# Retention and softplus feed-forward on one core: weight pieces in the order of use, one rest in four on GpSimd, two early constants' loads apart, and three idle products between the first two steps

## The chip, the cores and the metric

The kernel runs on one core of a Trainium2 chip. The metric is the device time of one execution in microseconds (us): the median of three runs of the kernel before is 893.17 us (893.16 to 894.15). The trace comes from one more execution, which took 891.85 us.

The engines are named as the profile names them: PE is TensorE's matmul, PEld its weight load, DVE is VectorE, ACT is ScalarE, POOL is GpSimd, SP is SyncE, on which all DMAs are issued here.

## The reference

```
scores = (q @ k.T) / sqrt(64)                   # 8 batches, 8 heads, 576 positions, head size 64
ret    = scores * gamma[h] ** (i - j)  (j <= i) # lower triangle with a decay per head
attn   = ret @ v
x      = attn, heads side by side               # 4608 tokens x 512
h      = x @ w_in                               # 512 x 2048
g      = max(h, 0) + log1p(exp(-|h|))           # softplus
out    = g @ w_out                              # 2048 x 512
```

All of it is float32. The weights are kept as pairs of a high and a low part, and so are x and g, so that each large product is three products in the fast format (high with low, low with high, high with high).

## The kernel before

**Attention** runs in steps: a step is one chunk of 128 tokens and two pairs of heads, so two steps make a chunk and there are 72 in all. The first eight steps are computed whole (`scores_whole`, `sums_whole`, `values_whole`), before any large product; the ninth follows half. For each the kernel loads a tile `raw` of 512 KB with k, q, k again and v, multiplies k by q (line 290), masks the result on DVE (`a_whole`, line 297), scales v on ACT (line 154), multiplies sums and values (lines 305, 327, 332), keeps a state per head that decays (lines 315 to 319), multiplies the output by a column of decays (`x`, line 344) and splits x into a high and a low part (lines 351, 352). The small constants (scales of v and the states' decay) and the columns of decays lie in the tiles of the first step, behind its data: `part0` holds k, q and the small ones, `part1` holds k, v and the columns. All constants are loaded a second time behind step 9, for the time after the opening.

**The feed-forward** runs in slots: slot i takes 512 tokens and the p-th of 16 strips of 128 hidden columns, `h` = 12 matmuls (line 367), softplus on ACT and DVE (lines 375 to 395), and one slot later `y` += 12 matmuls for the output (line 407). PE's order in a slot is: in odd slots the small products of one attention step, then `h(i)`, then `y(i-1)`. `y(i-1)` reads the low part of g first, which line 395 writes.

**The weights** come in 32 pieces of 512 columns as 64-bit floats. A piece is scaled on ACT (`weight_p`, line 440), its low word on DVE (`weight_t`, line 447), both are joined on DVE (`weight_b`, line 453), the high part is rounded on ACT (`weight_c`, line 461) and the rest is subtracted on DVE (`weight_d`, line 466). `weight_dl` also issues the load of the piece four further on. Pieces alternate: the strip of w_in, then the strip of w_out, of p = 0, 1, 2. Pieces 0 to 3 are loaded in the opening, 0 and 1 are finished there, and slot i works on pieces 2 + 2i and 3 + 2i: the rest of the first stands before the softplus sum (line 387), the rest of the second behind it. So in slot i the first `weight_dl` finishes the strip of w_in that `h(i+1)` reads, and the second the strip of w_out for `y(i)`.

The order on every engine is that of the code, written by hand; no planner sets it. Three idle products on a tile of ones (line 493) stand on PE ahead of the first scores.

Of the kernel before, what the change touches and what calls it, by code (L numbers as in the profile page):

```python
# [19 lines left out]
P = 128  # L20
# [20 lines left out]
START_WEIGHTS = 3  # L41
OPENING = 3
NOPEN = AHEAD + 2
CHUNKS = 9
FIRST_HALF = NF // 2
WBUFS = 4
NPIECE = 2 * NF
HI, LO = 0, 1
TERMS = ((LO, HI), (HI, LO), (HI, HI))


# [12 lines left out]
def retention_softplus_ffn(ctx: ExitStack, tc, first, whole, others, consts, w, out):  # L64
# [20 lines left out]

    parts = [openp.tile([P, n], F32, name=f"part{i}") for i, n in enumerate((4 * C + SMALL, 4 * C + NPAIR * C))]
    consts_sb = const.tile([P, NCONST], F32, name="consts_sb")
    mask = const.tile([P, HC], F32, name="mask")

    def constants(small, columns):  # L90

        return small[:, 0:H], small[:, H:SMALL], columns.rearrange("p (s c) -> p s c", s=NPAIR)

    constant = [constants(parts[0][:, 4 * C:], parts[1][:, 4 * C:])]
# [8 lines left out]
    place_weights(wpool, FIRST_HALF)  # L103

# [16 lines left out]
    def load_step(m):  # L121

        if m == 0:
            at = 0
            for x in parts:
                nc.sync.dma_start(x, first[:, at:at + x.shape[1]])
                at += x.shape[1]
            k, q = parts[0][:, 0:2 * C], parts[0][:, 2 * C:4 * C]
            kp, v = parts[1][:, 0:2 * C], parts[1][:, 2 * C:4 * C]
        else:  # L130
            if m < NOPEN:
                r = openp.tile([P, 8 * C if m < FIRST else RAW], F32, name=f"raw{m}")
                nc.sync.dma_start(r, whole[m - 1] if m < FIRST else others[m - FIRST])
                keys, qv = r[:, 0:KEYS], r[:, KEYS:]
            else:
                keys = rawp.tile([P, KEYS], F32, tag="keys", name="keys")
                nc.sync.dma_start(keys, others[m - FIRST][:, 0:KEYS])
                place = later["odd"] if m >= 2 * CHUNKS and m // 2 % 2 else rawp
                qv = place.tile([P, RAW - KEYS], F32, tag="qv", name="qv")
                nc.sync.dma_start(qv, others[m - FIRST][:, KEYS:])  # L140
            k, kp, q, v = keys[:, 0:2 * C], keys[:, 2 * C:], qv[:, 0:-2 * C], qv[:, -2 * C:]
        live[m] = {n: x.rearrange("p (s c) -> p s c", s=2) for n, x in dict(k=k, q=q, kp=kp, v=v).items()}

    def scale_values(m):

        if m >= NSTEP:
            return
        v = live[m]["v"].rearrange("p s (h d) -> p (s h) d", h=2)
        f = constant[0][0][:, 4 * (m % 2):4 * (m % 2) + 4]
# [46 lines left out]
    def states_out(m):  # L196
# [21 lines left out]
        if follows:  # L218
            s = att.tile([P, 2, D], F32, tag="s", name="s", bufs=4)
            if between is None:  # L220
                nc.vector.tensor_copy(s, sum1)
            else:
                nc.vector.tensor_add(s, sum1, between)  # L223
            f = constant[0][1][:, 2 * (m % 2):2 * (m % 2) + 2]
            nc.gpsimd.tensor_mul(s, s, f.unsqueeze(2).broadcast_to([P, 2, D]))  # L225
            states[m % 2] = s
# [82 lines left out]
    def state_whole(m):  # L309
        before = states.get(m % 2)  # L310
        live[m]["before"] = before
        total = live[m]["T"].rearrange("p (s d) -> p s d", s=2)
        s = att.tile([P, 2, D], F32, tag="s", name="s", bufs=4)
        if before is None:
            nc.vector.tensor_copy(s, total)
        else:
            nc.vector.tensor_add(s, total, before)
        f = constant[0][1][:, 2 * (m % 2):2 * (m % 2) + 2]
        nc.gpsimd.tensor_mul(s, s, f.unsqueeze(2).broadcast_to([P, 2, D]))
        states[m % 2] = s  # L320
# [15 lines left out]
    def values_out(m, rest):  # L336
# [6 lines left out]
        if m < FIRST:  # L343
            nc.vector.tensor_mul(x, L["O"], constant[0][2][:, pr:pr + 2])
        else:
            nc.vector.tensor_mul(x.rearrange("p s (t c) -> p s t c", t=2),  # L346
                                 L["O"].rearrange("p t (s c) -> p s t c", s=2),
                                 constant[0][2][:, pr:pr + 2].rearrange("p s (t c) -> p s t c", t=2))

# [9 lines left out]
    def hidden_mm(i, tag, cols=slice(0, T)):  # L359
# [5 lines left out]
        for a, b in TERMS:  # L365
            for kt in range(NKT):
                nc.tensor.matmul(h, ws[p][:, a, kt * P:(kt + 1) * P], xt[:, b, kt, cols],  # L367
                                 start=(n == 0), stop=(n == 3 * NKT - 1))
# [28 lines left out]
    def output_mm(i):  # L397
# [4 lines left out]
        for tt in range(CPU):  # L402
            y = ys[u][tt]
            for n, (a, b) in enumerate(TERMS):
                g = parts[tt * len(parts) // CPU]
                at = tt % (CPU // len(parts)) * P
                nc.tensor.matmul(y, g[:, a, at:at + P], ws[p][:, b, PIECE:],  # L407
                                 start=(p == 0 and n == 0), stop=(p == NF - 1 and n == 2))
# [18 lines left out]
    def load_weight(n):  # L427
        if n < NPIECE:
            wl[n] = wst.tile([P, PIECE, 2], I32, tag="wst", name="wst", bufs=WBUFS)
            nc.sync.dma_start(wl[n].rearrange("p c a -> p (c a)"), w[n // 2, n % 2])  # L430

# [23 lines left out]
    def weight_dst(n):  # L455
        cols = slice((n % 2) * PIECE, (n % 2 + 1) * PIECE)
        return ws[n // 2][:, HI, cols], ws[n // 2][:, LO, cols]

# [3 lines left out]

    def weight_d(n):
        if n in wl:
            head, rest = weight_dst(n)
            nc.vector.tensor_sub(rest, wl.pop(n)[:, :, 1].bitcast(F32), head.bitcast(F32))  # L466
# [24 lines left out]
    idle = ps_val.tile([P, 2, T], F32, tag="val", name="idle")  # L491
    for n in range(OPENING):
        nc.tensor.matmul(idle[:, 0, 0:2 * C], fill[:, 0:P], fill[:, 0:2 * C], start=True, stop=True)

# [8 lines left out]
    for m in range(2):  # L503
        next_scores(m)
        scale_values(m)
        masked_whole(m)
# [32 lines left out]
    ps_y = ctx.enter_context(tc.tile_pool(name="ps_y", bufs=1, space=PSUM, side="right"))  # L539
    constant[0] = constants(consts_sb[:, 0:SMALL], consts_sb[:, SMALL:])  # L540

# [3 lines left out]
    for i in range(NSLOT):  # L545
# [48 lines left out]
        if step and n < NPIECE:  # L594
# [6 lines left out]
            if m == NOPEN:  # L601
                open_pools.close()
                place_weights(ctx.enter_context(tc.tile_pool(name="wpool2", bufs=1)), NF)
        weight_c(n)
        weight_dl(n)
        gs[i] = [softplus_split(ab)]
# [84 lines left out]
```

## Time and profile before

| what | value |
|---|---|
| median of 3 runs | 893.17 us |
| the profiled execution | 891.85 us |
| its span, first to last instruction | 890.1 us |
| PE busy | 879.6 us (99%) |
| DVE, ACT, POOL busy | 460.1, 440.6, 144.1 us |
| mean granted TensorE clock | 0.998 of full speed |

The table gives totals over the whole span. The change lies in the opening (0 to about 23 us) and in the stretch in which the weights are still being prepared (to about 120 us), so the rows further down are from there. A timeline row gives the start, the time that it took, engine, line, operation, tiles and count, and in brackets how long the engine had been idle before and what ended that.

### The profile page before, as it was taken

What the parts mean: (1) busy time and instruction counts of PE and PEld (TensorE: products, weight loads), DVE (VectorE), ACT (ScalarE), POOL (GpSimd) and SP (SyncE); (2) the same over time, 40 slices, a digit from 0 to 9 for tenths busy, and PEclk for the clock granted to TensorE, in tenths of its full rate; (3) what the DMA queues carried; (4) which work ended last, traced back from release to release, by engine and by line L of the source; (5) the groups of instructions that cost most, each with busy time, mean ns of one, the idle gap of its engine ahead of it and who ended that gap; (6) DMA issues with size and microseconds to landing.
All of it is one profiled execution on the core that took longest, in us unless ns stands there. A gap on an engine that the chain in (4) does not pass through costs nothing.

```text
span 890.1 us, 18133 instructions
## 1 busy us (share of the span) xinstructions
PE 879.6 (99%) x7634; PEld 723.8 (81%) x7634; DVE 460.1 (52%) x875; ACT 440.6 (49%) x771; POOL 144.1 (16%) x265
## 2 busy tenths in 40 slices
PE   8999999999999999999999999999999999999998
PEld 6777778888888888888888888888888888888886
DVE  5898864445444454455444454444444544434333
ACT  6777854444544454444444454444444544444444
POOL 4221222111111111111111111111111111000000
PEclk9999999999999999999999999999999999999999
DMA  9666623111310121112111131012111211001001
GB/s 364 193 216 221 218 69 113 54 55 54 102 47 23 41 101 54 55 55 101 55 54 54 55 102 54 26 41 90 54 54 54 101 55 54 2 1 48 0 1 48
DMA packets 29313, 69.86 MB, mean 78 GB/s; under 512 B 3248, under 2 KB 3248, under 8 KB 29232
## 3 DMA queue, kind: packets, MB, share of 16 engines
q1 hardware_dynamic: 29232, 68.71, 22.9%
q8 instruction: 60, 0.98, 0.5%
q14 instruction: 21, 0.17, 0.1%
HBM read 59.26 MB, written 9.44 MB: 77 GB/s over the span
## 4 chain that ended last, share of the span: by engine, by line
PE 93%; DVE 3%; ACT 1%; DMA 1%; issue 0%; SPq 0%; DVEq 0%
PE h L367 43%; PE y L407 42%; PE sums L174 2%; PE bank L158 2%; PE bank L230 2%; PE bank L242 1%; DVE w L466 1%; DMA raw<-whole 1%; DVE g L395 1%; PE pair L290 1%; DMA wst<-w 1%; PE bank L327 0%; PE bank L305 0%; ACT ab L377 0%; ACT ab L376 0%
## 5 line engine op out<-in xcount | busy, mean ns | idle before, releaser
L367 PE MATMUL h<-xt,w 128*128 128x512 f32 (+1 forms) x1740 | 420.5, 391 | 1.9 <-DVE w L466 1.3
L407 PE MATMUL y<-w,g 128*128 128x512 f32 x1728 | 415.9, 390 | 1.2 <-DVE g L395 1.2
L407 PEld LDWEIGHTS y<-w,g 128*128 128x128 f32 x1728 | 323.7, 188 | 71.0 <-DVE g L395 4.0
L367 PEld LDWEIGHTS h<-xt,w 128*128 128x128 f32 x1740 | 322.1, 188 | 70.0 <-DVE w L466 1.7
L375 ACT ACTIVATE ab<-h 128x512 f32<-128x512 f32 (+1 forms) x145 | 86.3, 595 | 252.0 <-PE h L367 252.0
L383 DVE TENSOR_SCALAR r<-h 128x512 f32<-128x512 f32 x125 | 86.4, 692 | 211.1 <-ACT ab L375 211.1
L391 ACT CAST g<-ab 128x512 fp32r<-128x512 f32 (+1 forms) x145 | 89.5, 617 | 106.1 <-DVE ab L387 104.9
L395 DVE TENSOR_TENSOR g<-ab,g 128x512 fp32r<-128x512 f32 (+1 forms) x145 | 103.1, 711 | 69.4 <-ACT g L391 68.0
L352 POOL TENSOR_TENSOR xt<-x,xt 128x256 fp32r<-128x256 f32 x71 | 54.2, 780 | 519.7 <-ACT xt L351 519.7
L387 DVE SCALAR_TENSOR_TENSOR ab<-r,ab 128x512 f32<-128x512 f32 x125 | 89.4, 715 | 79.6 <-ACT ab L377 79.6
L376 ACT ACTIVATE ab<-ab 128x512 f32<-128x512 f32 (+1 forms) x145 | 91.2, 629 | 4.6
L377 ACT ACTIVATE ab<-ab 128x512 f32<-128x512 f32 (+1 forms) x145 | 91.2, 629 | 4.7
L351 ACT CAST xt<-x 128x256 fp32r<-128x256 f32 x72 | 27.1, 405 | 56.8 <-DVE x L346 55.4
L151 POOL TENSOR_TENSOR qv<-qv,consts_sb 128x256 f32<-128x256 f32 x61 | 41.3, 676 | 52.0 <-DMA qv<-others 51.6
L225 POOL TENSOR_TENSOR s<-s,consts_sb 128x128 f32<-128x128 f32 x55 | 24.2, 440 | 62.3 <-DVE s L223 50.1
L158 PE MATMUL bank<-qv,keys 64*64 64x64 f32 x976 | 34.0, 222 | 0.0
L346 DVE TENSOR_TENSOR x<-bank,consts_sb 128x256 f32<-128x256 f32 x64 | 24.6, 419 | 17.8 <-PE sums L174 12.3
L174 PEld LDWEIGHTS sums<-qv,keys 64*64 64x64 f32 x768 | 26.5, 134 | 8.5 <-issue 8.5
L230 PE MATMUL bank<-a,qv 64*64 64x64 f32 x976 | 32.9, 218 | 0.0
L158 PEld LDWEIGHTS bank<-qv,keys 64*64 64x64 f32 x976 | 29.4, 134 | 3.5 <-issue 3.5
L174 PE MATMUL sums<-qv,keys 64*64 64x64 f32 x768 | 32.0, 221 | 0.0
L230 PEld LDWEIGHTS bank<-a,qv 64*64 64x64 f32 x976 | 29.9, 135 | 0.4 <-issue 0.4
(84 smaller groups left out, 444.2 us busy)
## 6 DMA issues: line engine op xcount, KB each, us to landing
qv<-others SPq DMA_DIRECT2D x61, 320.0 KB, 4.1
wst<-w SPq DMA_DIRECT2D x32, 512.0 KB, 4.2
keys<-others SPq DMA_DIRECT2D x61, 256.0 KB, 3.5
out<-osb SPq DMA_DIRECT2D x36, 256.0 KB, 2.4
raw<-whole SPq DMA_DIRECT2D x7, 512.0 KB, 8.3
raw<-others SPq DMA_DIRECT2D x3, 576.0 KB, 10.7
part<-first SPq DMA_DIRECT2D x1, 512.0 KB, 3.7
part<-first SPq DMA_DIRECT2D x1, 262.0 KB, 2.7
```

The lines of the kernel that those rows point to most:

```text
L158: nc.tensor.matmul(L["S"][rows[t], h, part[s]], L["k"][rows[h], s, part[t]], L["q"][rows[h], s, part[t]], start=True, stop=True, skip_grou ...
L174: nc.tensor.matmul(L["T"][rows[h], t, part[s]], L["kp"][rows[t], s, rows[h]], L["v"][rows[t], s, rows[h]], start=True, stop=True, skip_gro ...
L230: nc.tensor.matmul(L["O"][rows[h], t, part[s]], L["v"][rows[t], s, rows[h]], L["a"][rows[t], h, s], start=clear, stop=L["states"][t] is No ...
L367: nc.tensor.matmul(h, ws[p][:, a, kt * P:(kt + 1) * P], xt[:, b, kt, cols], start=(n == 0), stop=(n == 3 * NKT - 1))
L375: nc.scalar.activation(ab, h, AF.Abs)
L376: nc.scalar.activation(ab, ab, AF.Exp, scale=-1.0)
L377: nc.scalar.activation(ab, ab, AF.Ln, bias=1.0)
L383: nc.vector.tensor_scalar_max(r, h, 0.0)
L387: nc.vector.scalar_tensor_tensor(ab, h, 0.0, ab, op0=ALU.max, op1=ALU.add)
L391: nc.scalar.copy(g[:, HI], ab)
L395: nc.vector.tensor_sub(g[:, LO], ab, g[:, HI].bitcast(F32))
L407: nc.tensor.matmul(y, g[:, a, at:at + P], ws[p][:, b, PIECE:], start=(p == 0 and n == 0), stop=(p == NF - 1 and n == 2))
```

## The change

Five edits, all in the first 120 us:

1. The first step's data come in two tiles of 256 KB without constants. The small constants (128 rows of 48 bytes) are a DMA of their own between the two, the columns of decays (256 KB) a DMA behind the load of step 1 and ahead of that of step 2. The second load of all constants behind step 9 goes.
2. Three more idle products (`BETWEEN`) follow the scores of step 0 on PE.
3. The weights' pieces are numbered in the order in which PE reads them: w_in of 0, w_in of 1, w_out of 0, w_in of 2, w_out of 1 and so on (`_piece`). The slots' code is the same, so the second `weight_dl` of slot i now finishes what `h(i+2)` reads, and the first one what `y(i)` reads.
4. In even slots the rest of the second piece is subtracted on POOL instead of DVE (`weight_dl(n, nc.vector if i % 2 else nc.gpsimd)`).
5. In the opening, pieces 1 and 2 are loaded behind the data of steps 6 and 8 instead of 5 and 7.

The start of SP's order, of which each row is one DMA; `part` is step 0, `raw` a later step, `wst` a weights' piece. Before:

```order
L126 DMA part_91<-first 128x524
L126 DMA part_92<-first 128x1024
L133 DMA raw_107<-whole 128x1024
L133 DMA raw_109<-whole 128x1024
L430 DMA wst<-w 128x1024
```

and now:

```order
L130 DMA part_91<-first 128x512
L130 DMA small<-consts 128x12
L130 DMA part_92<-first 128x512
L138 DMA raw_117<-whole 128x1024
L135 DMA columns<-consts 128x512
L138 DMA raw_120<-whole 128x1024
L435 DMA wst<-w 128x1024
```

The half of the second tile that held the columns has moved behind step 1, and one short DMA has come in between.

DVE in slot 0, from the join of piece 3 on. In the names of before, `w_96` is the tile of both strips of p = 1. Before:

```order
L447 TENSOR_SCALAR wst<-wst 128x512
L466 TENSOR_TENSOR w_96<-wst,w_96 128x512
L387 SCALAR_TENSOR_TENSOR ab<-h,ab 128x512
L466 TENSOR_TENSOR w_96<-wst,w_96 128x512
L395 TENSOR_TENSOR g<-ab,g 128x512
L453 SCALAR_TENSOR_TENSOR wst<-wst 128x512
```

and now, where each piece has a tile of its own (`w_98` is w_out of 0, `w_99` w_in of 2):

```order
L452 TENSOR_SCALAR wst<-wst 128x512
L470 TENSOR_TENSOR w_98<-wst,w_98 128x512
L392 SCALAR_TENSOR_TENSOR ab<-h,ab 128x512
L400 TENSOR_TENSOR g<-ab,g 128x512
L458 SCALAR_TENSOR_TENSOR wst<-wst 128x512
```

The rest between the softplus sum and the rest of g has gone from DVE.

POOL in the same place. Before:

```order
L151 TENSOR_TENSOR raw_131<-raw_131,part_91 128x256
L207 COPY sx<-s 64x128
L225 TENSOR_TENSOR s<-s,consts_sb 128x128
L151 TENSOR_TENSOR raw_444<-raw_444,consts_sb 128x256
L352 TENSOR_TENSOR xt_555<-x,xt_555 128x2x128
```

and now:

```order
L156 TENSOR_TENSOR raw_142<-raw_142,small 128x256
L470 TENSOR_TENSOR w_99<-wst,w_99 128x512
L212 COPY sx<-s 64x128
L230 TENSOR_TENSOR s<-s,small 128x128
L156 TENSOR_TENSOR raw_457<-raw_457,small 128x256
L357 TENSOR_TENSOR xt_568<-x,xt_568 128x2x128
```

The rest stands ahead of the copy of a state; the same comes back in each of the eight even slots up to slot 14.

The core of the diff:

```
-OPENING = 3
+OPENING, BETWEEN = 3, 3
+def _piece(p, side):
+    if side == IN:
+        return max(2 * p - 1, 0)
+    return min(2 * p + 2, NPIECE - 1)
...
-            ws.append(pool.tile([P, 2, 2 * PIECE], F32R, name=f"w{len(ws)}"))
+            ws.append(pool.tile([P, 2, PIECE], F32R, name=f"w{len(ws)}"))
...
-            at = 0
-            for x in parts:
-                nc.sync.dma_start(x, first[:, at:at + x.shape[1]])
-                at += x.shape[1]
+            for x, y in ((parts[0], first[0]), (small, consts[:, 0:SMALL]), (parts[1], first[1])):
+                nc.sync.dma_start(x, y)
...
+            if m == 2:
+                nc.sync.dma_start(columns, consts[:, SMALL:])
...
-    def weight_dl(n):
+    def weight_dl(n, engine=nc.vector):
         if n in wl:
-            weight_d(n)
+            weight_d(n, engine)
             load_weight(n + WBUFS)
...
-    first_weights = {2: (0,), 5: (1,), 7: (2,), 8: (3,)}
+    first_weights = {2: (0,), 6: (1,), 8: (2, 3)}
...
-    nc.sync.dma_start(consts_sb, consts)
...
     for m in range(2):
         next_scores(m)
+        if m == 0:
+            steady(BETWEEN)
         scale_values(m)
         masked_whole(m)
...
         weight_c(n)
-        weight_dl(n)
+        weight_dl(n, nc.vector if i % 2 else nc.gpsimd)
```

## Rows read from the trace of the kernel before

**Rows 1.** The page's head: span, and PE's busy time.
```profile
span 890.1 us, 18133 instructions
PE 879.6 (99%) x7634; PEld 723.8 (81%) x7634; DVE 460.1 (52%) x875; ACT 440.6 (49%) x771; POOL 144.1 (16%) x265
```

**Rows 2.** Busy time by stretch: PE, PEld, DVE, ACT, POOL, granted clock, DMA share, GB/s.
```profile
5.10:8.50 3.40, 1.70 (x42) 1.10 (x36) 1.38 (x2) 2.29 (x9) 0.00 (x0) 1.00 1.01 374
8.50:11.90 3.40, 3.40 (x50) 2.60 (x48) 1.94 (x5) 2.23 (x10) 1.51 (x3) 0.50 1.02 419
11.90:22.50 10.60, 10.60 (x239) 8.69 (x232) 8.79 (x20) 8.70 (x30) 6.49 (x12) 1.00 1.02 414
...
37.40:113.70 76.30, 75.06 (x666) 59.29 (x665) 69.32 (x127) 59.52 (x102) 18.28 (x25) 1.00 0.64 209
```

**Rows 3.** Timeline of PE in the opening.
```profile
1.52 2.93 PE L493 MATMUL idle<-fill 128*128 128x256 f32 x6 [1.52 <-DVE fill L476]
4.38 0.99 PE L290 MATMUL pair<-part 64*64 64x128 f32 x16
7.07 0.67 PE L290 MATMUL pair<-raw 64*64 64x128 f32 x16 [1.71 <-DMA raw<-whole]
...
8.49 1.13 PE L290 MATMUL pair<-raw 64*64 64x128 f32 x16
...
11.03 1.08 PE L290 MATMUL pair<-raw 64*64 64x128 f32 x16
```

**Rows 4.** Timeline of ACT in the opening: scaling v of step 3.
```profile
10.84 1.06 ACT L154 ACTIVATE raw<-raw,part 128x64 f32<-128x64 f32 x4 [1.17 <-DMA raw<-whole]
```

**Rows 5.** Timeline of PE around `h(1)`.
```profile
28.97 3.04 PE L367 MATMUL h<-xt,w 128*128 128x512 f32 x12 [1.28 <-DVE w L466]
31.84 2.88 PE L407 MATMUL y<-w,g 128*128 128x512 f32 x12
```

**Rows 6.** Timeline of ACT in slots 0 and 1: `weight_c(3)`, `weight_c(4)`, `h(1)`'s first step.
```profile
28.85 0.65 ACT L461 CAST w<-wst 128x512 fp32r<-128x512 f32 x1
...
31.69 0.68 ACT L461 CAST w<-wst 128x512 fp32r<-128x512 f32 x1 [0.20 <-DVE wst L453]
32.27 0.59 ACT L375 ACTIVATE ab<-h 128x512 f32<-128x512 f32 x1
```

**Rows 7.** Timeline of DVE in slot 0.
```profile
29.58 0.68 DVE L466 TENSOR_TENSOR w<-wst,w 128x512 fp32r<-128x512 f32 x1
30.36 0.69 DVE L395 TENSOR_TENSOR g<-ab,g 128x512 fp32r<-128x512 f32 x1
```

**Rows 8.** What PEld waited for from 29 to 125 us: us, times, longest.
```profile
PEld y L407 <- DVE g L395: 4.0, 7, 0.6
```

**Rows 9.** What ACT waited for from 37.4 to 114 us.
```profile
ACT ab L375 <- PE h L367: 1.4, 6, 0.3
```

**Rows 10.** Timeline of DVE in slot 3: the softplus sum of an odd slot.
```profile
46.47 0.69 DVE L387 SCALAR_TENSOR_TENSOR ab<-h,ab 128x512 f32<-128x512 f32 x1 [0.66 <-ACT ab L377]
```

**Rows 11.** Timeline of all engines in slot 4, an even one.
```profile
52.23 0.92 POOL L352 TENSOR_TENSOR xt<-x,xt 128x256 fp32r<-128x256 f32 x1
52.48 1.22 DVE L466 TENSOR_TENSOR w<-wst,w 128x512 fp32r<-128x512 f32 x1
...
53.11 0.67 ACT L461 CAST w<-wst 128x512 fp32r<-128x512 f32 x1
53.21 0.64 POOL L207 COPY sx<-s 64x128 f32<-64x128 f32 x1
...
54.99 0.69 DVE L395 TENSOR_TENSOR g<-ab,g 128x512 fp32r<-128x512 f32 x1
```

**Rows 12.** Groups on POOL by shape: count, busy us, mean ns, idle before.
```profile
L352 POOL TENSOR_TENSOR xt<-x,xt 128x256 fp32r<-128x256 f32 x71 | 54.2, 780 | 519.7 <-ACT xt L351 519.7
L151 POOL TENSOR_TENSOR qv<-qv,consts_sb 128x256 f32<-128x256 f32 x61 | 41.3, 676 | 52.0 <-DMA qv<-others 51.6
...
L319 POOL TENSOR_TENSOR s<-s,part 128x128 f32<-128x128 f32 x8 | 3.2, 400 | 9.1 <-DVE s L315 8.0 <-DVE s L317 1.0
```

More of the change, by code (lines that the diff above doesn't have):

```diff
@@ L48 @@
 HI, LO = 0, 1
+IN, OUT = 0, 1
 TERMS = ((LO, HI), (HI, LO), (HI, HI))
+def _piece(p, side):
+    if side == IN:
+        return max(2 * p - 1, 0)
+    return min(2 * p + 2, NPIECE - 1)
 def _chunk_kind(ch):
@@ L83, in retention_softplus_ffn @@
     ps_open = psum_pools.enter_context(tc.tile_pool(name="ps_open", bufs=2, space=PSUM, side="right"))
-    parts = [openp.tile([P, n], F32, name=f"part{i}") for i, n in enumerate((4 * C + SMALL, 4 * C + NPAIR * C))]
-    consts_sb = const.tile([P, NCONST], F32, name="consts_sb")
+    parts = [openp.tile([P, 4 * C], F32, name=f"part{i}") for i in range(2)]
+    small = const.tile([P, SMALL], F32, name="small")
+    columns = const.tile([P, NPAIR * C], F32, name="columns")
     mask = const.tile([P, HC], F32, name="mask")
-    def constants(small, columns):
-        return small[:, 0:H], small[:, H:SMALL], columns.rearrange("p (s c) -> p s c", s=NPAIR)
-    constant = [constants(parts[0][:, 4 * C:], parts[1][:, 4 * C:])]
+    constant = small[:, 0:H], small[:, H:SMALL], columns.rearrange("p (s c) -> p s c", s=NPAIR)
     ws = []
@@ L148, in scale_values @@
         v = live[m]["v"].rearrange("p s (h d) -> p (s h) d", h=2)
-        f = constant[0][0][:, 4 * (m % 2):4 * (m % 2) + 4]
+        f = constant[0][:, 4 * (m % 2):4 * (m % 2) + 4]
         if m >= AHEAD:
@@ L343, in values_out @@
         if m < FIRST:
-            nc.vector.tensor_mul(x, L["O"], constant[0][2][:, pr:pr + 2])
+            nc.vector.tensor_mul(x, L["O"], constant[2][:, pr:pr + 2])
         else:
@@ L455, in weight_dst @@
     def weight_dst(n):
-        cols = slice((n % 2) * PIECE, (n % 2 + 1) * PIECE)
-        return ws[n // 2][:, HI, cols], ws[n // 2][:, LO, cols]
+        return ws[n][:, HI], ws[n][:, LO]
     def weight_c(n):
@@ L461, in weight_c, with weight_d @@
             nc.scalar.copy(weight_dst(n)[0], wl[n][:, :, 1].bitcast(F32))
-    def weight_d(n):
+    def weight_d(n, engine=nc.vector):
         if n in wl:
             head, rest = weight_dst(n)
-            nc.vector.tensor_sub(rest, wl.pop(n)[:, :, 1].bitcast(F32), head.bitcast(F32))
-    def weight_dl(n):
+            engine.tensor_sub(rest, wl.pop(n)[:, :, 1].bitcast(F32), head.bitcast(F32))
+    def weight_dl(n, engine=nc.vector):
         if n in wl:
-            weight_d(n)
+            weight_d(n, engine)
             load_weight(n + WBUFS)
-    first_weights = {2: (0,), 5: (1,), 7: (2,), 8: (3,)}
+    first_weights = {2: (0,), 6: (1,), 8: (2, 3)}
     fill = moe.tile([P, T], F32, tag="ab", name="fill")
@@ L491, in retention_softplus_ffn, with steady @@
     idle = ps_val.tile([P, 2, T], F32, tag="val", name="idle")
-    for n in range(OPENING):
-        nc.tensor.matmul(idle[:, 0, 0:2 * C], fill[:, 0:P], fill[:, 0:2 * C], start=True, stop=True)
+    def steady(n):
+        for _ in range(n):
+            nc.tensor.matmul(idle[:, 0, 0:2 * C], fill[:, 0:P], fill[:, 0:2 * C], start=True, stop=True)
+    steady(OPENING)
     def next_scores(m):
@@ L539, in retention_softplus_ffn @@
     ps_y = ctx.enter_context(tc.tile_pool(name="ps_y", bufs=1, space=PSUM, side="right"))
-    constant[0] = constants(consts_sb[:, 0:SMALL], consts_sb[:, SMALL:])
     by_chunks = 2 * (2 * CHUNKS - AHEAD) + 1
@@ L664 @@
     w_out = w_out.reshape(NF, P, PIECE)
+    pieces = [None] * NPIECE
+    for p in range(NF):
+        pieces[_piece(p, IN)], pieces[_piece(p, OUT)] = w_in[p], w_out[p]
     gamma = 1.0 - 2.0 ** (-5.0 - np.arange(H, dtype=np.float64))
@@ L674 @@
     arrays = {
-        "first": np.concatenate([k, q, vsc, gchp, kp, v, decp], axis=1).astype(np.float32),
+        "first": np.stack([np.concatenate([k, q], axis=1), np.concatenate([kp, v], axis=1)]),
         "whole": whole[1:],
@@ L678 @@
         "consts": np.concatenate([vsc, gchp, decp], axis=1).astype(np.float32),
-        "w": np.stack([w_in, w_out], axis=1),
+        "w": np.stack(pieces),
     }
```

17 lines of the change are left out of this document (8 added, 9 removed).

## The prediction

> **What bounds the kernel now.** I read the page's head first: PE is busy 879.6 of 890.1 us [rows 1]. So what can be won is where PE waits or runs at the lower clock, and the change only reaches the first 120 us; behind them the work on PE is the same, and the order on every engine too. Second, the busy times by stretch [rows 2]. From 5.1 to 8.5 us PE works half of the time while the DMA engines are full (share 1.01), so data bound it. From 8.5 to 11.9 it is busy throughout, but the granted clock is 0.50, the lower of its two levels. From 11.9 to 22.5 it is busy 10.60 of 10.60 us at 1.00: what PE gains or loses before 11.9 is carried to the end of the opening. From 37.4 to 113.7 it is busy 75.06 of 76.30 us, and DVE 69.32. Third, the timelines and waits of those places, which give the terms below.
>
> The profiled execution took 891.85 us, 1.75 more than its span; the median of the runs shown is 893.17, or 1.32 above it. I work out differences against the profiled execution and put them on the median.
>
> **Opening: constants apart, products in the gap.** PE multiplies step 0 from 4.38 to 5.37, then waits until the data of step 1 are there at 7.07, an idle time of 1.71 us [rows 3]. After this gap the clock falls at 8.5, and the next two groups of scores take 1.13 and 1.08 us where the one at 7.07 took 0.67.
>
> The columns behind step 1 put 256 KB less ahead of its data. At the 374 GB/s of that stretch [rows 2] this is 0.70 us: 7.07 becomes 6.37. The short DMA takes some of it back. No row shows rows of 48 bytes; its bounds are nothing and the same 0.70 as the 256 KB transfer. I take 0.1, nearer to the low end because it has 6 KB. The Trainium skill, "DMA: Bandwidth & Descriptors", Specifications, says that transfers under 512 bytes fall short of the line rate, through read-modify-write; it gives no time, and no run here shows it yet. By it the upper bound would be the nearer one, and the gain below would go.
>
> The three products are six instructions. At the start six took 2.93 us at the lower level [rows 3], so at the full one half of that, 1.47. From 5.37 they end at 6.84, or at 8.30 if the level is still the lower one. The scores at 4.38 are in between (0.99 against 0.67 and 1.13), so the level had changed by their end, and I take 6.84. The scores of step 1 start then, 0.23 earlier than before, and PE is no longer idle for longer than the data of steps 2 and 3 make it.
>
> What this is worth is decided by the data of step 3, which are behind as many bytes as before. ACT waits for them until 10.84 [rows 4], PE starts on them at 11.03 and ends at 12.11 [rows 3]. At full clock PE is there waiting at 10.84, or 10.94 with the short DMA, and ends at about 11.67 (0.67, and 0.06 to start). The gain is 0.44, and I take 0.4; its bounds are 0.5 without the short DMA, and a loss of 0.4 if that costs its whole 0.70 and the products end late. The later steps' data have no bytes more in front, and steps 6 and 8 have a piece less; the pieces that come later are read long after. The second load of the constants sat in a queue on which nobody waits.
>
> **Order of the pieces.** `h(1)` waits 1.28 us for the rest of its piece [rows 5]. In the new order that piece is finished in the opening, so `h(1)` starts 1.28 earlier. What is late next is `y(0)` and then `y(1)`: PE needs the low part of g, and that comes from a chain in which `h(1)` has no part. Piece 3 is rounded on ACT at 28.85, the rest of g(0) is on DVE from 30.36 to 31.05 [rows 7], behind it the join of piece 4, then `weight_c(4)` on ACT at 31.69, which waits for DVE, then the softplus of `h(1)` at 32.27 [rows 6]. `h(1)` had ended at 32.01. With `h(1)` at 30.7 the softplus still comes at 32.27, so of the 1.28 us nothing reaches `y(1)`. The other pieces are early by more than a slot. I cost the order at 0, with bounds of 0 and a gain of 1.28.
>
> **The rest on POOL.** Eight rests leave DVE, some 0.68 us each [rows 7]. In an even slot, that rest ran at 29.58 to 30.26 while ACT made the high part of g; the rest of g could not start before 30.36 anyway. So it was hidden and its removal gains nothing there. The wait that PE does have, 4.0 us in 7 times [rows 8], is behind odd slots, whose rest stays on DVE. There DVE has been idle for 0.66 us ahead of its softplus sum [rows 10]: not its load, but the chain from the end of `h` through ACT sets the time, and ACT is waiting for `h` in 6 such slots (1.4 us in all [rows 9]). DVE's free time in even slots ends as longer idling ahead of the odd ones.
>
> On POOL no row has this shape. From 400 ns for 128 columns and 780 for 256, another 380 for each 128 [rows 12], 512 columns take 1.54 us; by the 676 ns of line 151, 1.23. I take 1.4. It starts when `weight_c` is done: in slot 0 at 29.50 [rows 6], and ends at 30.95. The rest of g would start at 30.36 on DVE. Rows 11 show what then happens: line 466 on DVE started at 52.48 during POOL's line 352, which ended at 53.15; it took 1.22 us in place of 0.68 and ended 0.55 after POOL. So g's rest ends at 31.50, 0.45 late. The Trainium skill, "SBUF — State Buffer", SBUF: two separate sides, has a rule for it that speaks against the change: VectorE with two SBUF inputs and GpSimd lock a shared port for a whole instruction and the other is blocked. This trace agrees (1.22 against 0.68). By its whole wording the sum is the same 0.45 late.
>
> The copy of a state now stands behind the rest on POOL; its turn comes between the rest of g and the join on DVE and costs at most its own 0.64 [rows 11]. I take 0.1. So `weight_c(4)`, the softplus of `h(1)` and `y(1)` come 0.55 later in the chain, less the opening's 0.4: +0.15 at `y(1)`.
>
> In the seven pairs of slots behind, the chain has more room. In slot 4 the rest would start on POOL at 53.85 (`weight_c` ends 53.78) and end at 55.25; g's rest, at 54.99 before, waits 0.26 and ends 0.12 later (55.80 against 55.68) [rows 11], with the copy about 0.2. ACT's idle time ahead of the next odd softplus is 1.4 / 6 = 0.23 [rows 9], which covers it. I take 0 for a pair, with bounds of 0 and, if the cover is gone, 0.3 each.
>
> **Sum.** -0.4 for the opening, 0 for the order, +0.55 in slot 0, 0 in the pairs: +0.15, so 892.0 for the profiled execution and 893.3 on the median. Its own range, from the bounds that hang on slot 0 and the opening: 892.2 to 894.5. A measurement of this kernel can tell about 0.2% (1.8 us) from no change; this is inside it.
>
> **Rivals.** *DVE was the bound after all (faster).* For it: DVE is busy 69.32 of 76.30 us, and the waits of PE are all put down to it. If less work on DVE ends the 4.0 us of waits ahead of `y` [rows 8], and the opening gives 0.4, the time is 893.17 - 4.4 = 888.8; with half of the waits 890.8. `h(1)`'s 1.28 would come on top where the chain behind it moves. Against it: the 0.66 us idle ahead of the odd sums, and that the odd rests stay.
>
> *POOL's rest holds the chain in every even slot (slower).* If it takes 2 us instead of 1.4 (its second operand may run slower than those of line 352), it ends at 55.85 in slot 4, g's rest at 56.40, 0.72 late, of which 0.23 are covered: 0.5 a pair. It decides from about 1.5 us on. Seven pairs make 3.5, slot 0 1.05 + 0.1, less 0.4: 897.4. For it: the lock, and that g's rest is on the way to `weight_c`. Against: the two groups of 256 columns, waits included, have means of 676 and 780 ns [rows 12], and twice the larger is 1.56.
>
> *The clock falls one stretch later.* At full clock PE has short idle times between 8.5 and 10.84 again. If it then runs at 0.50 for as long as it did, 3.4 us, but in the stretch where PE is the bound, it does 3.4 x 0.67 / 1.13 = 2.0 us of work and loses 1.4; the 0.4 goes as well: 895.1. For it: a gap of 1.71 us came before the fall. Against: after 1.28 us without work ahead of `h(1)` the next 12 matmuls still took 2.88 us [rows 5], no more than elsewhere; and the 3.40 us of work between 8.5 and 11.9 shrink by half at most, so the idle time there is at most 1.7 us, in two pieces, for step 2 and step 3.
>
> *The order is not what PE feels*, that is, the change does what it says and nothing is late by it, is part of the forecast.
>
> **Chances.** Forecast 0.61, faster by DVE 0.18, slower by POOL 0.11, clock 0.10. Of the clock's case half is above 894.96 and half is not. So faster by over 0.2% (below 891.38) 0.17, slower (above 894.96) 0.16, within 0.67; the missing 0.01 of the faster case is half of its waits or less. The range runs from 890.8, the half of the waits, to 895.3, which takes in the clock and leaves out the slower case and the lower half of the faster one.
>
> **What would show it.** Right: scores of steps 1 to 3 on PE at about 0.67 us and a granted clock of 1.00 from 8.5 to 11.9; `h(1)` without its wait, but a new wait of some 0.3 to 0.8 us ahead of `y(0)` or `y(1)` on line 400; the POOL rest at 1.2 to 1.55 us, g's rest beside it at over 0.8; the distance from `y(1)` to `y(13)` as before. Wrong: a shorter distance between `y` of odd slots (the first rival), a POOL rest over 1.5 us with ACT no longer waiting for `h` (the second), or 0.50 in a row after 11.9 (the third).

## The result and the profile after

The changed kernel takes 894.18 us (median of 20 runs, 893.2 to 895.2) against 892.87 for the kernel before beside it: a ratio of 1.0016 with a 95% interval of 1.0009 to 1.0022, so 1.4 us (0.8 to 2.0) slower. In a second session it was 893.99 against 893.27, 1.0008 (0.9999 to 1.0017), so the loss is clear of no change in the first session alone. The forecast was 893.3, or 0.15 us slower: the direction is right, and forecast and time both lie inside the 1.8 us that the prediction called no change. But the time is 0.9 us above the forecast, and two steps of the forecast failed. In brackets behind a ratio stands its interval, here and below.

The head of its page, against [rows 1], and its stretches in the columns of [rows 2], with one more ahead:

```profile
span 892.2 us, 18158 instructions
PE 881.2 (99%) x7640; PEld 724.5 (81%) x7640; DVE 457.5 (51%) x867; ACT 440.5 (49%) x771; POOL 154.8 (17%) x273
```

```profile
0.00:5.10 5.10, 3.58 (x22) 2.57 (x22) 0.48 (x1) 1.28 (x1) 1.27 (x9) 1.00 0.57 149
5.10:8.50 3.40, 3.40 (x36) 2.27 (x32) 0.74 (x2) 2.03 (x8) 0.00 (x0) 1.00 0.96 356
8.50:11.90 3.40, 2.19 (x48) 1.56 (x46) 2.58 (x6) 1.45 (x6) 1.39 (x3) 1.00 1.02 414
11.90:22.50 10.60, 10.23 (x224) 8.23 (x226) 7.85 (x19) 8.96 (x31) 6.36 (x10) 1.00 1.03 412
...
37.40:113.70 76.30, 74.30 (x662) 58.65 (x661) 66.23 (x120) 59.53 (x104) 27.12 (x30) 1.00 0.65 212
```

The clock no longer falls at 8.5 us: 1.00 where [rows 2] have 0.50. But PE is now idle for 1.2 us there. From 37.4 on DVE has 3.1 us less to do and POOL 8.8 more, and PE, at 74.30 against 75.06, waits more, not less. The first 5.1 us moved 149 GB/s; in before they moved 216.

PE's scores and ACT's step 3 in the opening, against [rows 3, 4]:

```profile
4.38 1.13 PE L295 MATMUL pair<-part 64*64 64x128 f32 x16
5.44 2.34 PE L497 MATMUL idle<-fill 128*128 128x256 f32 x6
7.72 0.67 PE L295 MATMUL pair<-raw 64*64 64x128 f32 x16
...
9.58 0.67 PE L295 MATMUL pair<-raw 64*64 64x128 f32 x16 [0.38 <-DMA raw<-whole]
...
12.14 0.67 PE L295 MATMUL pair<-raw 64*64 64x128 f32 x16 [1.07 <-DMA raw<-whole]
...
12.03 1.06 ACT L159 ACTIVATE raw<-raw,small 128x64 f32<-128x64 f32 x4 [1.20 <-DMA raw<-whole]
```

The groups of scores of steps 1 to 3 take 0.67 us each, as forecast. Step 1's group starts behind the products, 0.2 us after its data. Those of steps 2 and 3 wait for data that come later than before: step 3's are there at 12.03 where [rows 4] have 10.84.

Slots 0 and 2, against [rows 5 to 7]: PE, then POOL, DVE and ACT.

```profile
28.82 3.02 PE L372 MATMUL h<-xt,w 128*128 128x512 f32 x12
32.78 2.99 PE L412 MATMUL y<-w,g 128*128 128x512 f32 x12 [0.94 <-DVE g L400]
...
43.05 1.32 POOL L470 TENSOR_TENSOR w<-wst,w 128x512 fp32r<-128x512 f32 x1 [2.57 <-PE bank L247]
...
31.57 1.07 DVE L400 TENSOR_TENSOR g<-ab,g 128x512 fp32r<-128x512 f32 x1 [0.69 <-ACT g L396]
...
43.81 1.11 DVE L400 TENSOR_TENSOR g<-ab,g 128x512 fp32r<-128x512 f32 x1 [0.69 <-ACT g L396]
...
45.65 0.67 ACT L465 CAST w<-wst 128x512 fp32r<-128x512 f32 x1 [0.73 <-DVE wst L458]
46.22 0.60 ACT L380 ACTIVATE ab<-h 128x512 f32<-128x512 f32 x1
```

`h(1)` starts behind its attention step without a wait; what is late instead is `y(0)`, by 0.94 us, for the low part of g. In slot 2 POOL's rest runs from 43.05 to 44.37 and g's rest beside it takes 1.11 us, not 0.69; ACT then waits 0.73 for the join before `weight_c`, and the next softplus stands behind it. The rests on POOL (count, shortest, median and longest in ns, first and last start), and PE's waits for g from 37.4 to 113.7 us (sum, times, longest), against [rows 8]:

```profile
L470 POOL TENSOR_TENSOR w<-wst,w x8: 1310/1314/1324, 30.8 to 119.9; 128x512 fp32r<-128x512 f32 x8
```

```profile
PEld y L412 <- DVE g L400: 4.5, 6, 1.0
```

**All profiles in one table.** The opening varies from execution to execution, so a difference of two spans isn't the worth of an edit. The columns, from each kernel's one profile: when the clock was at 1.00; when ACT began on step 3's data; the first weight load of `h(0)`; from there to `y(1)`; from `y(1)` to `y(13)`; from `h(0)` to the end; and the median time of the kernel (us).

| kernel | clock 1.00 from | step 3 | h(0) | to y(1) | y(1)-y(13) | h(0)-end | median |
|---|---|---|---|---|---|---|---|
| before | 5.09, not 8.51-11.92 | 10.84 | 23.36 | 14.05 | 76.27 | 866.74 | 892.5-893.4 |
| order_alone | 13.3 | 11.00 | 24.70 | 14.14 | 76.27 | 866.82 | 893.01 |
| weights_alone | 13.98 | 11.55 | 25.31 | 14.38 | 76.91 | 867.71 | 892.87 |
| weights_again | 12.92 | 11.26 | 24.65 | 14.36 | 77.23 | 867.99 | 893.36 |
| after | 7.06 | 12.03 | 24.57 | 14.34 | 76.83 | 867.63 | 894.18 |
| after_again | 4.86 | 12.71 | 25.31 | 14.34 | 76.59 | 867.35 | 893.99 |
| a_vector | 6.94 | 11.73 | 24.44 | 13.87 | 76.96 | 867.23 | 893.33 |
| opening_alone | 5.92 | 11.93 | 24.63 | 13.87 | 76.92 | 867.21 | 893.46 |
| no_between | 13.24 | 11.38 | 24.43 | 14.35 | 77.17 | 867.93 | 894.05 |
| small_back | 5.16 | 11.12 | 23.82 | 14.33 | 76.83 | 867.52 | 893.46 |
| rest_behind | 10.12 | 10.80 | 23.66 | 13.51 | 74.65 | 864.66 | 890.83 |
| best | 4.75, not 11.58-14.99 | 11.69 | 25.15 | 13.51 | 75.28 | 865.24 | 891.66 |
| load_ahead | 13.04 | 11.36 | 24.84 | 13.51 | 74.12 | 864.04 | 889.96 |
| all_pool | 5.38, not 94.13-97.54 | 10.39 | 23.32 | 13.52 | 84.00 | 873.91 | 899.57 |

Before's opening stands in seven of them (before, order_alone, both weights, rest_behind, load_ahead, all_pool). `h(0)` starts at 23.3 to 23.7 in the three where the clock was up by 10.12, and at 24.65 to 25.31 in the four where it came at 12.9 or later. Not all of that is the clock: the data of step 3 came at 10.39 to 10.84 in the three and at 11.00 to 11.55 in the four. From these data to `h(0)` it took 12.5 to 12.9 us in the three and 13.4 to 13.8 in the four. The profile of before was one of the quick ones, and its 893.17 - 891.85 = 1.32 below the median fits that.

### The profile page after: what moved, and what is told of

Read it like the earlier page. It is cut to its first block, busy times and chain, and to the rows that moved or that the text cites. A ratio compares the mean times of both kernels' runs of the same rounds, so it can differ in the third digit from the quotient of the medians.

```text
span 892.2 us, 18158 instructions
## 1 busy us (share of the span) xinstructions
PE 881.2 (99%) x7640; PEld 724.5 (81%) x7640; DVE 457.5 (51%) x867; ACT 440.5 (49%) x771; POOL 154.8 (17%) x273
## 4 chain that ended last, share of the span: by engine, by line
PE 91%; DVE 4%; ACT 2%; DMA 1%; issue 1%; SPq 0%; DVEq 0%
PE h L372 41%; PE y L412 41%; PE sums L179 2%; PE bank L163 2%; PE bank L235 2%; PE bank L247 1%; DMA raw<-whole 1%; DVE g L400 1%; DVE ab L392 1%; DVE wst L458 1%; DMA wst<-w 1%; ACT ab L381 1%; ACT ab L382 1%; DVE w L470 0%; ACT ab L380 0%
## 5 line engine op out<-in xcount | busy, mean ns | idle before, releaser
L372 PEld LDWEIGHTS h<-xt,w 128*128 128x128 f32 x1740 | 322.1, 188 | 68.4 <-ACT w L465 0.8
L400 DVE TENSOR_TENSOR g<-ab,g 128x512 fp32r<-128x512 f32 (+1 forms) x145 | 105.7, 729 | 74.2 <-ACT g L396 73.5
L156 POOL TENSOR_TENSOR qv<-qv,small 128x256 f32<-128x256 f32 x61 | 39.5, 648 | 51.9 <-DMA qv<-others 51.8
L351 DVE TENSOR_TENSOR x<-bank,columns 128x256 f32<-128x256 f32 x64 | 24.6, 419 | 17.8 <-PE sums L179 12.3
L230 POOL TENSOR_TENSOR s<-s,small 128x128 f32<-128x128 f32 x56 | 24.7, 441 | 45.6 <-DVE s L228 35.7
```

The costliest lines, as they stand in the source:

```text
L372: nc.tensor.matmul(h, ws[_piece(p, IN)][:, a, kt * P:(kt + 1) * P], xt[:, b, kt, cols], start=(n == 0), stop=(n == 3 * NKT - 1))
L400: nc.vector.tensor_sub(g[:, LO], ab, g[:, HI].bitcast(F32))
```

## Experiments

**The opening alone, the order and POOL's rest, the order alone.** From the changed kernel, for opening_alone:

```
-    if side == IN:
-        return max(2 * p - 1, 0)
-    return min(2 * p + 2, NPIECE - 1)
+    return 2 * p + side
...
-        weight_dl(n, nc.vector if i % 2 else nc.gpsimd)
+        weight_dl(n)
```

weights_alone is the kernel before with the order of use and POOL's rest; order_alone takes from it `nc.vector if i % 2 else nc.gpsimd`.

> Only the opening of the change (constants apart, products in the gap, first weights' loads moved); pieces in the old order, all rests on DVE. Theory A (the two added short loads take issue time and two of the eight places in SP's queue, so every later load lands later): step 3's data land at 12.0 us instead of 10.8, h(0) starts at 24.2 to 24.6 instead of 23.4, y(13) is late by the same, and the time is 0.8 to 1.2 us over before. Theory B (the opening costs nothing, the loss is the POOL rest): h(0) at 23.0 to 23.4 and the time that of before.

> Only the weights' part of the change (order of use, even slots' rest on POOL); the opening of before. Theory A (POOL's rest holds the rest of g in slot 0 and in some pairs): h(0) at 23.4 as before, h(1) at 27.7 (28.97 before), y(1) at 37.7 (37.4), y(13) at 114.3 to 114.7 (113.7); time 0.6 to 1.0 us over before. Theory B (the loss is the opening alone): y(1) at 37.4 or earlier, y(13) not after 113.7, time that of before or less.

> Only the order of use; all rests on DVE, opening of before. Theory A (h(1) is not on the path, the chain through ACT and DVE is): h(1) starts at 27.7, 1.28 us earlier, y(1) still at 37.4, pairs of 12.7 us, time that of before within 0.2 us. Theory B (the order gains what h(1) waited): y(1) and y(13) 0.5 to 1.3 us earlier and the time 0.5 to 1.3 us less.

The ratios to before are 0.9998 (0.9989 to 1.0008), 0.9998 (0.9989 to 1.0008) and 0.9996 (0.9987 to 1.0005). No part alone can be told from no change, so the 0.6 to 1.2 us that the first cases of opening_alone and weights_alone expected did not show in their times. The profiles tell more. The order moves nothing: it takes 14.14 us from `h(0)` to `y(1)` and 76.27 from there to `y(13)`, against 14.05 and 76.27. POOL's rest on top of it does what was forecast for slot 0. The rows are ACT's `weight_c` and softplus of `h(1)`, first of order_alone, then of weights_alone:

```profile
33.03 0.67 ACT L467 CAST w<-wst 128x512 fp32r<-128x512 f32 x1 [0.22 <-DVE wst L460]
33.60 0.59 ACT L382 ACTIVATE ab<-h 128x512 f32<-128x512 f32 x1
```

```profile
32.32 1.09 DVE L402 TENSOR_TENSOR g<-ab,g 128x512 fp32r<-128x512 f32 x1 [0.69 <-ACT g L398]
...
34.14 0.67 ACT L467 CAST w<-wst 128x512 fp32r<-128x512 f32 x1 [0.72 <-DVE wst L460]
34.71 0.60 ACT L382 ACTIVATE ab<-h 128x512 f32<-128x512 f32 x1
```

From `h(0)` the softplus comes 8.90 us later in the one and 9.40 in the other: 0.50, as ACT's wait grew from 0.22 to 0.72; of it 0.24 is left at `y(1)`. The first pair of slots behind takes 12.91 for 12.72 us, as in all six profiles with the rest of even slots alone on POOL (12.89 to 12.95); with all rests at their place on DVE it takes 12.70 to 12.72 in four. The pair from `y(5)` on takes 13.14 for 12.70, but opening_alone has 13.28 there without POOL: that loss is not POOL's alone.

**The short load taken back** (small_back): the twelve columns ride behind k and q again.

```
-            for x, y in ((parts[0], first[0]), (small, consts[:, 0:SMALL]), (parts[1], first[1])):
-                nc.sync.dma_start(x, y)
+            for x in parts:
+                ...
+            nc.gpsimd.tensor_copy(small, parts[0][:, 4 * C:])
```

> The changed kernel with the small constants back behind k and q of step 0 (rows of 2096 bytes) and copied from there by POOL, so that the DMA with rows of 48 bytes goes; the columns still apart. Theory A1 (the 48-byte load costs its turn in the queue): step 1's data land at 7.0 instead of 7.5, step 3's at 11.4 instead of 12.0, h(0) 0.5 us earlier than in the changed kernel (24.1). Theory A2 (smaller transfers or the columns ahead of step 2 cost it): step 3's data still at 11.9 to 12.0, h(0) at 24.6.

It took 893.46 us, a ratio of 1.0001 (0.9992 to 1.0011). Step 3's data are there at 11.12 and `h(0)` starts at 23.82, 0.75 before the changed kernel. The direction holds, the size less so: with the short load step 3's data came at 11.38 to 12.71 (five profiles), without it at 11.12 and 11.69 (this run and best), so 0.55 earlier in the mean, with overlap.

**The products of a constant taken away** (no_between): `BETWEEN = 0`.

> The changed kernel without the three products of a constant behind the scores of step 0; they feed nothing, so the outputs are the same. Theory D1 (the products hold the clock, so that it does not fall between 8.5 and 11.9 us; without them it falls or rises late): a stretch of granted clock 0.50 or lower than 1.00 behind 7 us, h(0) at 25.0 to 26.0 in place of 24.57, the time 0.4 to 1.4 us above the changed kernel, 894.6 to 895.6. Rival D2 (data bound the opening and the clock is no part of it): scores of step 1 start when its data are there, at 7.5, h(0) at 24.2 to 24.6, the time within 0.4 us of the changed kernel, though the granted clock may be lower in a row.

It took 894.05 us, a ratio of 1.0018 (1.0008 to 1.0028), as the changed kernel. Its clock came up only at 13.24; with the products it was up by 4.75 to 7.06 in all six profiles and fell again in one (best). And still `h(0)` starts at 24.43, no later than with most of them, and the time is the second case's. That does not show that the clock is worth nothing: step 3's data came at 11.38 here, earlier than in the four other profiles with this opening (11.73 to 12.71). From these data to `h(0)` it took 13.05 us; in the five profiles with the products in which the clock stayed up, 12.54 to 12.71. So by one profile against five the clock was worth 0.3 to 0.5 us behind the data, and the earlier data hid it. The times, with intervals of 0.9 us to either side, can't show so little.

**POOL's rest taken away from the changed kernel** (a_vector): `weight_dl(n)` in place of the choice of engine.

> The changed kernel with all rests on DVE, nothing else: its opening and its order of use stay. It computes all of the reference. Theory F1 (the rest on GpSimd costs 0.9 us, as the two profiles with before's opening showed: 867.71 against 866.82 from h(0) to the end): h(0) to the end 866.7 to 866.9, y(1) to y(13) 76.2 to 76.4, no pair over 12.8, and the time 0.7 to 1.1 below the changed kernel, 893.1 to 893.5. Rival F2 (those profiles differ by chance, and the times of the two kernels, 892.87 with GpSimd and 893.01 without, say that it costs nothing): time 893.9 to 894.4, a pair over 12.8 in it as well.

It took 893.33 us, a ratio of 0.9998 (0.9989 to 1.0007). That is 0.85 us under the changed kernel's median, which the first case expected; of the changed kernel's two ratios, 1.0016 and 1.0008, only the first has an interval that doesn't overlap with this one. The profile splits it differently: 0.47 less to `y(1)`, the first pair 12.70 for 12.93, but pairs of 13.35 and 12.96 from `y(5)` on, where DVE waits for a piece:

```profile
72.47 0.43 DVE L452 TENSOR_SCALAR wst<-wst 128x512 int32<-128x512 uint32 x1 [1.45 <-DMA wst<-w]
```

In the changed kernel the same wait is 1.01 us, in order_alone 0.33. The piece wasn't asked for late: its load left at 67.33 and took 5.12 us to land, in order_alone at 67.96 and 4.00. So "no pair over 12.8" and 866.7 to 866.9 us from `h(0)` to the end (867.23) were wrong: late pieces cost some 0.1 to 0.8 us, with POOL's rest and without. What makes them take longer isn't settled.

**The rest of all slots on POOL** (all_pool): in weights_alone `weight_dl(n, nc.gpsimd)`.

> Before's opening with the order of use, and the second rest of every slot on GpSimd (16 or so in place of 8). It computes all of the reference. Theory C1 (GpSimd's rest of 1.3 us delays g's rest on DVE through what they share, as in slot 0, where it took 1.07 in place of 0.69 us): in odd slots nothing covers that delay, so PE's waits grow and a pair takes 12.8 to 13.2 us; time 894 to 896. Rival C2 (what leaves DVE in odd slots is on the way to g, 0.68 us, and is gained nearly whole): pairs of 12.2 to 12.5, time 889.5 to 891.5.

It took 899.57 us, a ratio of 1.0077 (1.0060 to 1.0093). The sign was the first case's, the price more than twice as large: pairs of slots took up to 15.07 us. (In this profile the clock was at 0.50 from 94.13 to 97.54, which is in the pair of 13.70 and not in the longest three.) Slot 4 on POOL and DVE, then what waited:

```profile
52.94 1.30 POOL L472 TENSOR_TENSOR w<-wst,w 128x512 fp32r<-128x512 f32 x1
54.20 0.73 POOL L359 TENSOR_TENSOR xt<-x,xt 128x256 fp32r<-128x256 f32 x1
54.90 1.76 POOL L472 TENSOR_TENSOR w<-wst,w 128x512 fp32r<-128x512 f32 x1
...
54.38 1.11 DVE L402 TENSOR_TENSOR g<-ab,g 128x512 fp32r<-128x512 f32 x1 [0.68 <-ACT g L398]
55.41 1.80 DVE L460 SCALAR_TENSOR_TENSOR wst<-wst 128x512 int32<-128x512 int32 x1
58.59 0.43 DVE L454 TENSOR_SCALAR wst<-wst 128x512 int32<-128x512 uint32 x1 [1.38 <-DMA wst<-w]
```

```profile
ACT wst L447 <- DMA wst<-w: 10.1, 4, 3.7
PEld y L414 <- DVE g L402: 8.4, 6, 2.9
```

Beside POOL the join takes 1.80 us (0.69 alone), POOL's own rest 1.76 (1.31). Their ends tell that they took turns: POOL's line 359 ends at 54.93, g's rest 0.56 behind it at 55.49, POOL's rest 1.17 behind that at 56.66, and the join 0.55 behind that at 57.21. So what a row shows beyond that is waiting. And the load of the next piece stands behind the rest: issued late, it lands late, and ACT waits 10.1 us for pieces. This second cost was not in this run's expectation.

**DVE's second rest behind g's** (rest_behind: from order_alone, all rests on DVE):

```
         weight_c(n)
-        weight_dl(n)
         gs[i] = [softplus_split(ab)]
         ...
         weight_b(n + 1)
+        weight_dl(n)
```

> The kernel before with its own opening, the order of use, and all rests on DVE, but the second rest of each slot stands behind the rest of g and the join of the next piece, instead of ahead of the softplus sum; legal only with the order of use, where that piece is read two slots later. It computes all of the reference. Theory B1: in odd slots the rest on DVE (0.68 us) is on the way from h to the low part of g, which PE then waits for; behind the rest of g it is off that way, so the waits of PE ahead of y in 37.4 to 113.7 us (4.0 us in 7 of its weight loads) shrink to under 1.5, a pair of slots takes 12.2 to 12.45 us in place of 12.7, and the time falls by 2 to 4 us, to 889.5 to 891.5. Rival B2 (DVE's sum of work is the bound, or the rest only moves into the way of the next slot): pairs stay at 12.6 to 12.75, the time within 1 us of before. Rival B3: the load behind that rest is issued later by some 2 us, lands too late for the split of the piece, and DVE waits for a DMA: pairs of 12.9 or more, 894 to 896.

It took 890.83 us, a ratio of 0.9978 (0.9967 to 0.9988): the first case, 2.0 us faster (1.1 to 2.9). PE's waits for g from 37 us on, 4.0 us in 7 times before [rows 8], are all but gone:

```profile
PEld y L414 <- DVE g L402: 0.3, 1, 0.3
```

The pairs take 12.2 to 12.4 us, except for two of 12.69 and 12.84. There PE waits for POOL, and POOL for a load:

```profile
64.57 1.01 POOL L158 TENSOR_TENSOR qv<-qv,consts_sb 128x256 f32<-128x256 f32 x1 [2.69 <-DMA qv<-others]
...
65.64 0.46 PE L181 MATMUL bank<-qv,keys 64*64 64x64 f32 x16 [0.25 <-POOL qv L158]
```

**Together with the short load taken back** (best: small_back with this move).

> The changed kernel with two edits: the small constants ride behind k and q of step 0 and are copied on GpSimd (one DMA less), and all rests are on DVE, the second of each slot behind the rest of g. It computes all of the reference. By A1 (the short load costs about 0.75 us of the opening) with B1 (the odd rest is on the way to g): h(0) at 23.6 to 24.0 us, pairs of 12.2 to 12.45, the time 889 to 891. By B2: pairs of 12.6 to 12.75 and 892 to 893.5, the POOL rest's 0.9 us given back and no more. By B3: 894 or more.

It took 891.66 us, a ratio of 0.9986 (0.9977 to 0.9994), not better than the move with before's opening. Three pairs took 12.7 to 12.9 us, with the same wait for qv, and `h(0)` started at 25.15, not at 23.6 to 24.0: step 3's data came at 11.69 and the clock was at 0.50 from 11.58 to 14.99. Neither case foresaw that.

**The next step's loads ahead of the slot's first piece** (load_ahead, from rest_behind):

```
+        if step and n < NPIECE and NOPEN <= m + 1 < NSTEP:
+            load_step(m + 1)
         weight_dl(n - 1)
         ...
             states_out(m)
-            if NOPEN <= m + 1 < NSTEP:
-                load_step(m + 1)
             scale_values(m + 1)
```

> The kernel with the second rest behind the rest of g (the run rest_behind), and the loads of the next step's keys and qv issued ahead of the slot's first weight load instead of behind it, so that they do not stand on SP behind its wait for DVE's first rest. It computes all of the reference. Theory E1: the two pairs of slots that still took 12.69 and 12.84 us there are those in which GpSimd waited 2.7 and 2.6 us for qv and PE then for GpSimd (0.25 and more ahead of the attention's products); with the loads earlier all seven pairs take 12.2 to 12.3, y(1) to y(13) shrinks from 74.65 to 73.2 or 73.8 us, and the time by another 0.8 to 1.4, to 889.4 to 890.2. Rival E2: the loads only change places, the piece behind them lands later and DVE or ACT waits for it: sum of the pairs 74.4 or more, the time as in rest_behind, 890.5 to 891.5.

It took 889.96 us, a ratio of 0.9963 (0.9949 to 0.9976): 3.3 us faster than before (2.1 to 4.6), below both kernels. Its interval overlaps with rest_behind's, so that it beats that run too is shown by the profile alone. The pairs take 12.29 to 12.43, 74.12 in sum against rest_behind's 74.65, a little over the expected 73.2 to 73.8. PE is busy throughout from 37.4 on, and what is left of the waits is small:

```profile
37.40:113.70 76.30, 76.30 (x674) 60.80 (x673) 70.44 (x131) 61.57 (x107) 19.86 (x27) 1.00 0.62 216
```

```profile
POOL qv L158 <- DMA qv<-others: 3.3, 5, 1.3
PEld y L414 <- DVE g L402: 2.0, 7, 0.4
```

**The changed kernel and weights_alone again, on one chip.**

> The changed kernel once more, timed on one chip with the run weights_again beside it, and with a second profile. Theory G1 (the parts add: the new opening costs 0 to 0.5 us and the rest on GpSimd about 0.9 behind h(0)): 893.6 to 894.4, and weights_again 893.3 to 894.1, so that the two are within 0.5 us of one another. Rival G2 (the rest on GpSimd costs only beside the new opening): 893.9 to 894.6 here and 892.5 to 893.0 there, 1.2 us or more apart. In the second profile G1 and G2 both expect h(0) within 0.5 of 24.57 us and h(0) to the end at 867.5 to 867.8.

> Before's opening with the order of use and one rest in four on GpSimd (the run weights_alone) once more, beside after_again. G1: 893.3 to 894.1, within 0.5 us of after_again. G2: 892.5 to 893.0, 1.2 us or more below it. Its second profile shows whether the start of h(0), 25.31 us in the first, belongs to the kernel or to the execution: by the kernel again 25.0 to 25.6; by the execution anywhere from 23.3 to 25.3 (the spread of the runs with this opening so far), with the rise of the clock at another time than 13.98; h(0) to the end in either case 867.5 to 867.9.

They took 893.99 and 893.36 us, 0.63 apart: between the two cases. The second profiles settle the spread: `h(0)` at 25.31 for 24.57, 24.65 for 25.31, with the clock up at other times, so this belongs to the execution. From `h(0)` to the end, 867.35 and 867.99 us lie 0.1 to 0.2 outside what was expected. What stays open: behind `h(0)` weights_alone has 1.0 to 1.3 us more than before, and its time is that of before in both sessions. Its two profiled executions were slow ones of their kernel (894.81 for a median of 892.87, 894.43 for 893.36), so that stretch may vary too.

## Why the prediction was right or wrong

**Data of the opening (failed).** The steps that failed are "7.07 becomes 6.37", the 0.1 for the short load, and step 3's data "behind as many bytes as before". Step 1's data were there at 7.53 (6.88 to 8.22 in the four profiles with this opening and the products), step 3's at 12.03 for the forecast's 10.94. With the mean of the seven profiles of before's opening at 11.03, and 12.10 of these four, 1.1 us were lost. The runs split it, by means of few profiles that overlap. With the columns apart but no short load (two profiles) step 1's data came at 6.77, 0.40 before the 7.17 of before's seven, for a forecast of 0.70; step 3's came at 11.41, already 0.4 late. With the short load (five profiles) step 1's came at 7.36 and step 3's at 11.96, later by another 0.6.

The step looked at bytes ahead of the data and not at the loads as instructions. Each takes SP 0.43 us and more to issue, so that step 1's load leaves at 2.18 for 1.72 and step 3's at 4.08 for 3.22, and the first 5.1 us move 149 GB/s for 216. That the later issue alone makes the data late is argued and not shown. As to the Trainium skill's rule in "DMA: Bandwidth & Descriptors", Specifications, that transfers under 512 bytes fall short of the line rate: the trace agrees, and prices it. A packet of 48 bytes took 11 ns, one of 2048 bytes 84 in the median; but the 128 short ones come to 1.4 us of engine time, or 0.09 us on 16 engines. So the 0.1 was right for the transfer itself, and what the short load cost, 0.55 to 0.6, has another cause.

**Products and clock (half right).** The clock held, in five of six profiles. The six instructions took 1.47 by forecast; 1.56 us in three profiles where the clock was up, 2.34 here, where the lower level lasted until 7.06. The gain of 0.4 did not come: `h(0)` starts in the mean at 24.74 in four profiles against 24.26 in before's seven, and the times (a_vector, opening_alone: 0.9998) show no difference. The late data took more than the gain. And behind the data it was lost again: step 3's scores take 0.67 for 1.08 us, but the main part of step 6's takes 1.16 where step 7's takes 0.66, and the trace names no cause for the idle time in it:

```profile
17.67 1.16 PE L295 MATMUL pair<-raw 64*64 64x128 f32 x14
...
20.02 0.66 PE L295 MATMUL pair<-raw 64*64 64x128 f32 x14
```

So it is in all five profiles with the products in which the clock stayed up (0.5 to 0.66 us), and in neither before nor no_between. From step 3's data to `h(0)` the changed kernel takes 12.54 us and before's profile 12.52. Measuring from one quick execution hid, besides, that before's opening is mostly slower than its profile.

**Order of the pieces (right).** The forecast was 0; measured from `h(0)` to the end it is 0.08 us. The chain through g, the join, `weight_c` and the softplus sets `y(1)`, and `h(1)`'s 1.28 us are not part of it.

**POOL's rest, slot 0 (right).** The rest was forecast at 1.4 us and took 1.31. g's rest was to end 0.45 late and the softplus 0.55; order_alone against weights_alone has 0.50 for the softplus, of which 0.24 is left at `y(1)`; 0.47 with the new opening (after against a_vector). The trace agrees with the locked port of the Trainium skill's "SBUF — State Buffer", SBUF: two separate sides: g's rest takes 1.07 to 1.11 us for 0.69 beside POOL, and in slots 0, 2 and 4 it ends 0.55 us behind POOL's.

**Pairs (mis-sized).** The forecast was 0; measured are 0.32 to 0.56 us in the changed kernel (76.59 and 76.83 for 76.27). The step that failed is slot 4 as the measure for all pairs. In the first pair 0.2 is POOL's: slot 2's g's rest lost 0.42, not slot 4's 0.12, and with ACT's cover of 0.23, as forecast, 0.2 came through. In slot 4 it took 0.77 us, and that pair (12.72 and 12.75) lost nothing, as forecast. The rest are late pieces.

**Rivals.** DVE's load was not the bound: 3.1 us less of it made no pair shorter. But the rival had the right engine. The odd rest's place ahead of g's was the wait, and moving it made the pairs 0.3 to 0.4 us shorter with DVE as busy as before (68.4 and 70.4 us, 69.3 in before). These runs moved the even slots' rests too; that the odd ones did it follows from where PE waited and wasn't tried apart. POOL in every slot came at 899.57, as the mechanism of the slower rival, though in odd slots. The clock did not fall later in either profile of the changed kernel; it did in best (11.58) and in all_pool (94.13).

**Sum.** Forecast -0.4 + 0.55 = +0.15. By the two profiles of after, +0.61 to +0.89 behind `h(0)`; with the time's +0.7 and +1.4 the opening has cost some 0 to 0.5. So the opening and the pairs both came out slower than forecast, and that the time lies in the range owes much to its width: 4.5 us, three times what was measured.

## What to carry to other kernels

Ask of an operation on a busy engine whether it is on the way to what the bound engine waits for, not how much it adds up to: moving each slot's second rest of 0.68 us behind the operation that PE waits for brought 2 us, taking eight such off the engine none. Count a load by its time to issue and not by its bytes alone, and look at what stands behind a waiting load. Where one profile is far from the median, find the stretch that varies before an edit there is priced from it. Where data set the pace, measure from the moment they arrive: else early data hide what an edit is worth.

## What was not expected of the hardware

SP's loads of after in the opening; data landed at 3.57, 3.74, 5.52, 7.51, 8.18, 9.45, 10.73 and 12.0 us.

```profile
4.08 2.73 SPq L138 DMA_DIRECT2D raw<-whole  x4
7.52 0.33 SPq L435 DMA_DIRECT2D wst<-w  x1
8.19 0.33 SPq L138 DMA_DIRECT2D raw<-whole  x1
9.46 0.33 SPq L138 DMA_DIRECT2D raw<-others  x1
10.74 1.60 SPq L435 DMA_DIRECT2D wst<-w  x2
```

```profile
SPq L138 <- DMA columns<-consts: 0.3, 1, 0.3
```

The twelfth load leaves at 7.52, when the fourth has landed (7.51), the thirteenth at 8.19 behind the fifth (8.18): eight are under way, and each further one waits for the landing of the one eight before it, though they have no data in common. In before it is the same (the twelfth at 8.29, the fourth landing at 8.28). It looks like a limit of the queue, but the trace shows a wait of the program: the loads report their landing on eight semaphores in turn, and the twelfth load's instruction itself waits for semaphore 105, the one that the fourth raises. kernel.py has no such wait; it came in when the program was built. Nor does it explain the late data of the opening: the loads of steps 1, 2 and 3 are the fourth, the sixth and the eighth, and none of them waits.

The same opening reached full clock between 5.09 and 13.98 us with the same instructions on PE ahead of it. `h(0)` differs by up to 2 us between these seven profiles; of the two furthest apart, all_pool and weights_alone, 1.16 of the 1.99 us are there already in the data of step 3, and 0.83 come behind them.
